# The third gate and value pair moved forward in a fused attention and feed-forward kernel, and ScalarE's masks moved behind its tanh

## The chip, the cores and the metric

The kernel runs on one core of one Trainium2 chip. The metric is device time in microseconds (us) of that core, the median of several executions. The core has five engines that work in parallel, each through its own list of instructions: TensorE (PE in the profile, with its weight loads as PEld) multiplies, VectorE (DVE) and ScalarE (ACT) work on elements, GpSimd (POOL) and SyncE (SP) issue loads and stores here. TensorE writes its results to PSUM, from where VectorE and ScalarE fetch them.

## The reference

A sliding-window attention with distance bias feeds a gated feed-forward block. Batch 8, 8 heads, sequence 576, head size 64, window 128; 4608 tokens of width 512, inner width 1536.

```python
scores = q @ k.T / sqrt(64) - slope[h] * abs(i - j)      # kept where 0 <= i - j < 128
attn = softmax(scores)
x = (attn @ v)                       # heads side by side: 4608 x 512
g = x @ w_gate                       # 4608 x 1536
silu = g * (1 / (1 + exp(-g)))
out = (silu * (x @ w_val)) @ w_out   # 4608 x 512
```

## The kernel before: the parts that matter here

Tokens are worked on in nine blocks of 512 (`n`), the inner width in twelve parts of 128 (`m`). A part has a gate multiplication `pg` and a value multiplication `pv`, each of four matmuls into one PSUM tile of 512 columns. `wide` makes one of them; columns may be done in pieces, and the tile stays in `early` until its last columns are in:

```python
OTHER = {(0, 0, "g"), (0, 0, "v"), (0, 1, "g"), (0, 1, "v")}

def wide(n, m, which, c1=512):
    w, ms = wg_sb if which == "g" else wv_sb, slice(m * P, (m + 1) * P)
    ps, c0 = early.pop((n, m, which), (None, 0))
    if ps is None:
        pool, tag = (ps_a, "a") if (n, m, which) in OTHER else (ps_f, "gv")   # "gv" has 3 buffers, "a" has 4
        ps = pool.tile([P, 512], FP32, name="p" + which, tag=tag)
    for kb in range(NKB):                                                     # NKB = 4
        nc.tensor.matmul(ps[:, c0:c1], w[:, kb, ms], xT[n][:, kb, c0:c1], ...)
    if c1 < 512:
        early[(n, m, which)] = (ps, c1)
    return ps
```

`gate` takes tanh on ScalarE (tile `tt`) and a product on VectorE (`uu`), `val` the product with the value on VectorE (`hT`). Both read PSUM:

```python
def gate(n, m, pg, c0=0, c1=512):
    ...
    nc.scalar.activation(tt, pg[:, c0:c1], AF.Tanh, scale=0.5)
    nc.vector.scalar_tensor_tensor(out=uu, in0=tt, scalar=..., in1=pg[:, c0:c1], op0=ALU.add, op1=ALU.mult)

def val(n, m, pv, c0=0, c1=512):
    ...
    nc.vector.tensor_mul(hT[n][:, m, c0:c1], acted[(n, m)][1][:, c0:c1], pv[:, c0:c1])

def gate_val(n, m):
    c0 = 384 if (n, m) in acted else 0
    gate(n, m, wide(n, m, "g"), c0)
    yield
    val(n, m, wide(n, m, "v"), c0)
    yield
```

The kernel opens with the attention of the first four pieces of 128 tokens, because the first weights arrive then. It multiplies the columns of block 0 as their tokens become ready, for the first three pairs (`begin` makes the pieces up to a column). Before the feed-forward loop starts, the first 384 columns of the first three pairs are in, and those of pairs 0 and 1 have been through `gate` and `val`:

```python
    begin(4, 3)
    gate(0, 0, early[(0, 0, "g")][0], 0, 384)
    x_transposed(FIRST - 1)
    val(0, 0, early[(0, 0, "v")][0], 0, 384)
    later_masks(0, 2)
    gate(0, 1, early[(0, 1, "g")][0], 0, 384)
    val(0, 1, early[(0, 1, "v")][0], 0, 384)
    begin(6, 3)
```

The masks (`m_reg`) are eight exponentials on ScalarE, one for each head. The later attention scores are multiplied with them. Two are made above, the other six between the first steps of the feed-forward loop, and `make_masks` copies them into three further tiles (`m_c`) later:

```python
def later_masks(n, many):
    for h in by_slot[n:n + many]:
        nc.scalar.activation(reg[:, slot(h), :], dist, AF.Exp, scale=-(2.0 ** (-8.0 * (h + 1) / H)))

    # in ffn(), for each block n
    for m in range(NMB):                         # NMB = 12
        for half, _ in enumerate(gate_val(n, m)):
            yield 1.0
            ...
        if n == 1:
            if m in (4, 6, 8, 10):
                for _ in project(0, m // 2 - 2, ps_f, "po", 1):
                    yield 1.0
    ...
    # in everything()
    with tc.manual_schedule(engines=ENGINES[MANUAL]):    # TensorE, VectorE, ScalarE in the order of the program
        first_tiles()
        steps = progress(ffn())
        while (at := next(steps)) < ALONE:               # ALONE = 8
            if at == 2.0:
                nc.scalar.copy(idm2, idm)
            if at in (1.0, 3.0, 4.0):
                later_masks(2 * (1, 3, 4).index(at) + 2, 2)
```

After step 8 a scheduler of the build chooses the order of the instructions on each engine from the dependences, up to step 60 (the end of block 1) on TensorE and throughout on the others. Attention of later tokens and the feed-forward blocks are then mixed. Attention has scores (`ps`, `psc`), exponentials (`ex`, `exc`), products with the masks, products with v (`av`), normalising (`rec`, `x`) and a transpose of x (`px`, copied to `xT`), which the gate of the next block needs. k and q are transposed through `pt`.

The projection of block 0 (`po`) begins with the last rows of `wo_sb`; these weights are loaded in two halves, the last rows first:

```python
def project(n, j, pool, tag, bufs):
    po = pool.tile([P, DM], FP32, name="po", tag=tag, bufs=bufs)     # one buffer
    for m0 in range(0, NMB, 4):
        for i in range(m0, m0 + 4):
            m = NMB - 1 - i if n == 0 else i
            nc.tensor.matmul(po, hT[n][:, m, j * P:(j + 1) * P], wo_sb[:, m, :], ...)
        if m0 + 4 == NMB:
            nc.scalar.mul(osb, po, 0.5)
            ...
    # the loads, on GpSimd's queue behind all other weights
    nc.gpsimd.dma_start(wo_sb[:, 6:12, :], wo2[:, 6:12, :])
    nc.gpsimd.dma_start(wo_sb[:, 0:6, :], wo2[:, 0:6, :])
```

Of the kernel before, what the change touches and what calls it, by code (L numbers as in the profile page):

```python
# [39 lines left out]
def slot(h):  # L40

    return 4 * (h // 4) + 2 * (h % 2) + (h % 4) // 2
# [9 lines left out]
def kernel(  # L52
# [15 lines left out]
    NMB = DFF // P  # L68
# [38 lines left out]
# [3 lines that stand above are left out]
# [282 lines left out]
# [5 lines that stand above are left out]
            pool, tag = (ps_a, "a") if (n, m, which) in OTHER else (ps_f, "gv")  # L397
            ps = pool.tile([P, 512], FP32, name="p" + which, tag=tag)
        for kb in range(NKB):
            nc.tensor.matmul(ps[:, c0:c1], w[:, kb, ms], xT[n][:, kb, c0:c1],  # L400
                             start=(kb == 0 and c0 == 0), stop=(kb == NKB - 1 and c1 == 512),
                             skip_group_check=(n == 0))
# [3 lines that stand above are left out]
# [4 lines left out]
    def gate(n, m, pg, c0=0, c1=512):  # L410

        if (n, m) not in acted:
            acted[(n, m)] = [supool.tile([P, 512], FP16, name=i, tag=i) for i in ("tt", "uu")]
        tt, uu = (t_[:, c0:c1] for t_ in acted[(n, m)])
        if (n, m) in by_silu:
            nc.scalar.activation(tt, pg[:, c0:c1], AF.Silu)
            return
        nc.scalar.activation(tt, pg[:, c0:c1], AF.Tanh, scale=0.5)  # L418
        nc.vector.scalar_tensor_tensor(out=uu, in0=tt, scalar=one if (n, m) == PIN else 1.0,  # L419
                                       in1=pg[:, c0:c1], op0=ALU.add, op1=ALU.mult)  # L420

    def val(n, m, pv, c0=0, c1=512):

        if n not in hT:
            hT[n] = hpool.tile([P, NMB, 512], FP16, name="hT", tag="hT")
        if (n, m) in by_silu:
            nc.vector.scalar_tensor_tensor(out=hT[n][:, m, c0:c1], in0=acted[(n, m)][0][:, c0:c1], scalar=2.0,
                                           in1=pv[:, c0:c1], op0=ALU.mult, op1=ALU.mult)
            return
# [8 lines that stand above are left out]
# [55 lines left out]
    def at_once(fs):  # L493
        for f in fs:
            f()
# [209 lines left out]
    def ffn():  # L705

        for n in range(NBLK):
            if n > 1:
                parts = chain(strassen(n - 1, 0), strassen(n - 1, 1))
            if n == 1:  # L710
                for j in range(PRE):
                    for _ in project(0, j, ps_f, "po", 1):
                        yield 1.0
            if n == SEVEN_FROM:
                break
            due, given = 0, 0
            for m in range(NMB):
                for half, _ in enumerate(gate_val(n, m)):
                    scored[0] = False
                    yield 1.0  # L720
                    due += n > 1 and 2 * m + half in AT
                    while due and not (scored[0] and given % 7 == 1):
                        next(parts)
                        due, given = due - 1, given + 1
                        yield 0.75
                    if n > 1:
                        for _ in range(1 + (len(later) > 3)):
                            if later:
                                later.pop(0)()
# [4 lines that stand above are left out]
                    if m in (4, 6, 8):  # L734
                        weight_sums(m // 2 - 2)
                if n > 0 and m >= 9:
                    (at_once if n == 1 and m < 11 else later.extend)(sums(n, m - 9))
                if n + 1 == SEVEN_FROM:
                    if m == SILU_AT:
                        attention_ends()  # L740
                        by_silu.update((n, i) for i in range(m + 1, NMB))
                    if m in (SILU_AT + 1, SILU_AT + 2):
                        later.extend(gate_val_weight_sums(m - SILU_AT - 1))
                    if m == SILU_AT:
                        later.extend(x_sums(n + 1))
            if n > 1:
                assert next(parts, 0) == 0
        ends = [strassen(NBLK - 1, t) for t in range(2)]
        final = ()
        for n, k, name, which in seven_steps():  # L750
            if k == 0 and n > SEVEN_FROM:
                assert next(parts, 0) == 0
                parts = chain(strassen(n - 1, 0), strassen(n - 1, 1))
            if n == SEVEN_FROM and k in (1, 3, 10, 17):
                later.extend(gate_val_weight_sums(2 + (k + 4) // 7))
            yield 0.5
            if k % 3 == 2 and k < 42:
                next(parts)
                yield 0.75
            if k == 20 and n + 1 < NBLK:  # L760
                later.extend(x_sums(n + 1))
            if k == 35:
                later.extend(sums(n, 0))
            if name == "fourth" and which is not None and which[1] > 3:
                if which == (NBLK - 1, 5):
                    at_once(final)
                else:
                    later.extend(sums(which[0], which[1] - 3))
            if n == NBLK - 1 and k == 40:
                final = sums(n, 2)  # L770
                later.append(final.pop(0))
            for _ in range(2 if len(later) > 4 or k >= 39 or k < 7 else 1):
                if later:
                    later.pop(0)()
            if n == NBLK - 1 and k == 41:
                next(ends[0])
                yield 0.75
        assert next(parts, 0) == 0 and not later

        for t in (1, 0, 1, 0, 0, 0, 1, 0, 0, 1, 1, 1, 1):  # L780
            next(ends[t])
            yield 0.75
# [155 lines left out]
    def progress(steps):  # L938
        total = 0.0
        for size in steps:  # L940
            total += size
            yield total

    def everything():
        nonlocal done
        base = 0
        busy(WARM)
        with tc.manual_schedule(engines=ENGINES[MANUAL]):
            first_tiles()
            done = FIRST  # L950
            steps = progress(ffn())
            while (at := next(steps)) < ALONE:
                if at == 2.0:
                    nc.scalar.copy(idm2, idm)
                if at in (1.0, 3.0, 4.0):
                    later_masks(2 * (1, 3, 4).index(at) + 2, 2)
        fixed = ExitStack()
        for step in steps:
            if step >= FIXED_FROM and fixed is not None:
                fixed.enter_context(tc.manual_schedule(engines=ENGINES["pe"]))  # L960
                fixed, held = None, fixed
            if step == MASKS_AT:
                make_masks()

            b1 = 24 + 3 * PRE

            lead = LEAD if done < X_DMA_FROM - 2 else LEAD + 4
            blk = (0 if step + LEAD < b1 else 1 if step + LEAD < 60
                   else min(NBLK - 1, 2 + int((step + lead - 60) // 34.5)))
            if step < b1:  # L970

                target = base + 1.25 * max(0, step - ALONE) + 1.5 * max(0, step - 16)
            elif step < 60:
                target = base + 32 + SECOND * 8 * (step - b1) / (60 - b1)
            else:
                target = 84 + (step - 57) * RATE / 34.5
            while (n_att < target or done < ready[blk]) and att_step():
                pass
        held.close()
# [33 lines left out]
```

The softmax here doesn't subtract the row's maximum and nothing guards it: scores larger than these inputs give would overflow.

## Time and profile before

| What | Value |
|---|---|
| Device time, median of 3 | 343.38 us (343.19 to 343.41) |
| Span of the profiled execution | 342.1 us, mean granted TensorE clock 0.999 |
| TensorE busy | 330.2 us (97%) |
| VectorE busy | 277.3 us (81%) |
| ScalarE busy | 207.0 us (61%) |
| GpSimd busy | 109.6 us (32%) |
| TensorE busy from 20 to 30 us | 9.20 of 10.00 |
| TensorE busy from 50 to 57 us | 6.56 of 7.00 |

Times in the profile are counted from the start of the span. A row of a timeline gives the start in us, the duration, the engine, the line in the kernel, the operation, what is written from what, and how many instructions were merged; in brackets stands the idle time of the engine just before, with what ended it. TensorE's matmuls overlap at their ends: four of 512 columns show a duration of about 1.03 us but follow each other at 0.86 us. So distances between starts tell more than durations.

### The profile page before, as it was taken

The numbers are of one execution on the slowest core, as the hardware profiler recorded it, in microseconds if no ns is written. First come the engines' busy times: TensorE is split into PE (matmuls) and PEld (weight loads), VectorE is DVE, ScalarE is ACT, GpSimd is POOL, SyncE is SP. The second block draws the span as 40 slices with busy tenths as digits, with TensorE's granted clock in tenths as the row PEclk, the third lists the DMA queues.
The fourth block names the chain that finished last, engine by engine and source line by source line (L and its number), as shares of the span: only waits on it lengthen the run. The fifth ranks groups of instructions, "written<-read, shape, count | busy, mean of one in ns | idle before, by whom it ended". The sixth has DMA issues, their size and how long they took to land.

```text
span 342.1 us, 7787 instructions
## 1 busy us (share of the span) xinstructions
PE 330.2 (97%) x2983; PEld 218.6 (64%) x2983; DVE 277.3 (81%) x652; ACT 207.0 (61%) x412; POOL 109.6 (32%) x136
## 2 busy tenths in 40 slices
PE   7999999999999999999999999999999999999994
PEld 3484445444455665566655655666788878888884
DVE  5477885999798779998899999999855975775683
ACT  3748676565765675666655557463477667676640
POOL 8978672649755176744017000000000000000000
PEclk9999999999999999999999999999999999999999
DMA  9999999999999999999959932041101101011024
GB/s 151 169 180 177 163 173 150 81 132 160 149 173 143 172 166 161 164 162 147 188 125 100 178 35 79 15 77 35 61 10 53 63 0 64 23 41 63 0 71 116
DMA packets 160037, 37.37 MB, mean 109 GB/s; under 512 B 147328, under 2 KB 155648, under 8 KB 160000
## 3 DMA queue, kind: packets, MB, share of 16 engines
q0 software_dynamic: 118336, 18.62, 84.5%
q1 hardware_dynamic: 40976, 17.64, 28.4%
q10 hardware_dynamic: 688, 0.62, 0.6%
q8 instruction: 23, 0.38, 0.5%
q14 instruction: 14, 0.11, 0.1%
HBM read 37.91 MB, written 9.44 MB: 138 GB/s over the span
## 4 chain that ended last, share of the span: by engine, by line
PE 75%; DVE 14%; ACT 6%; issue 3%; DMA 2%; SPq 0%; DVEq 0%
PE po L535 16%; PE pg L400 14%; PE pv L400 14%; PE gX L627 8%; PE av L348 4%; PE gY L627 4%; PE ps L280 3%; PE po L454 2%; PE p L535 2%; DVE hT L430 2%; PE gZ L627 2%; ACT tt L418 2%; ACT ex L286 2%; DVE uu L419 2%; DMA stage<-in_q_dram 2%
## 5 line engine op out<-in xcount | busy, mean ns | idle before, releaser
L400 PE MATMUL pv<-xT,wv_sb 128*128 128x512 f16 (+2 forms) x320 | 76.5, 358 | 0.6 <-DVE uu L419 0.3
L400 PE MATMUL pg<-xT,wg_sb 128*128 128x512 f16 (+2 forms) x320 | 75.8, 358 | 0.3 <-DVE xT L376 0.2
L418 ACT ACTIVATE tt<-pg 128x512 f16<-128x512 f32 (+2 forms) x70 | 41.3, 590 | 47.7 <-PE pg L400 46.6
L286 ACT ACTIVATE ex<-ps 128x512 f16<-128x512 f32 x96 | 50.0, 606 | 10.5 <-PE ps L280 10.5
L419 DVE SCALAR_TENSOR_TENSOR uu<-tt,pg 128x512 f16<-128x512 f16 (+2 forms) x69 | 45.9, 666 | 10.5 <-ACT tt L418 10.3
L430 DVE TENSOR_TENSOR hT<-uu,pv 128x512 f16<-128x512 f16 (+2 forms) x70 | 46.6, 666 | 3.0 <-PE pv L400 1.3
L185 POOL DMA_DIRECT2D va<-in_v_dram x40 | 34.3, 862 | 36.7 <-PE av L348 30.4
L400 PEld LDWEIGHTS <-wv_sb 128*128 128x128 f16 x320 | 28.3, 98 | 25.1 <-issue 3.2
L535 PEld LDWEIGHTS <-hT 128*128 128x128 f16 x384 | 37.0, 98 | 10.6 <-issue 0.8
L400 PEld LDWEIGHTS <-wg_sb 128*128 128x128 f16 x320 | 28.2, 98 | 23.3 <-issue 2.2
L191 POOL DMA_DIRECT2D kn<-in_k_dram x39 | 33.2, 854 | 21.7 <-DMA kT<-kn 11.2
L191 POOL DMA_DIRECT2D qn<-in_q_dram x39 | 33.3, 860 | 15.3 <-DMA va<-in_v_dram 8.8
L535 PEld LDWEIGHTS <-S 128*128 128x128 f16 x288 | 27.3, 98 | 9.0 <-issue 1.4
L292 DVE TENSOR_TENSOR ex<-ex,m_reg 128x1024 f16<-128x1024 f16 x42 | 28.8, 686 | 3.0 <-ACT ex L286 3.0
L351 DVE TENSOR_TENSOR x<-av,rec 128x256 f16<-128x256 f32 x72 | 28.8, 420 | 0.4
L535 PE MATMUL po<-T,S 128*128 128x256 f16 x192 | 26.5, 273 | 0.6 <-DVE S L490 0.3
L535 PE MATMUL po<-T,hT 128*128 128x256 f16 x192 | 26.0, 273 | 0.1
L679 DVE TENSOR_TENSOR hT<-s,v 128x512 f16<-128x512 f16 x18 | 7.6, 423 | 18.5 <-ACT s L678 18.5
L320 ACT ACTIVATE exc<-psc 128x512 f16<-128x512 f32 x40 | 21.3, 609 | 1.9 <-PE psc L316 1.9
L348 PEld LDWEIGHTS <-ex 128*128 128x128 f16 x384 | 17.4, 97 | 4.6 <-issue 1.2
L348 PE MATMUL av<-va,ex 128*128 128x65 f16 x384 | 19.3, 193 | 0.7 <-ACT ex L286 0.7
L280 PE MATMUL ps<-qT,kT 64*128 64x256 f16 x192 | 16.7, 272 | 0.4 <-DVE qT L223 0.2
(134 smaller groups left out, 537.0 us busy)
## 6 DMA issues: line engine op xcount, KB each, us to landing
out_dram<-osb SPq DMA_DIRECT2D x32, 256.0 KB, 2.6
va<-in_v_dram POOLq DMA_DIRECT2D x32, 128.0 KB, 8.1
qn<-in_q_dram POOLq DMA_DIRECT2D x31, 128.0 KB, 8.6
kn<-in_k_dram POOLq DMA_DIRECT2D x31, 128.0 KB, 8.9
wg_sb<-in_moe_w_gate_dram POOLq DMA_DIRECT2D x6, 256.0 KB, 7.7
wv_sb<-in_moe_w_val_dram POOLq DMA_DIRECT2D x6, 256.0 KB, 8.1
wo_sb<-in_moe_w_out_dram POOLq DMA_DIRECT2D x2, 768.0 KB, 9.7
kn<-in_k_dram POOLq DMA_DIRECT2D x8, 64.0 KB, 7.6
```

The lines of the kernel that those rows point to most:

```text
L185: nc.gpsimd.dma_start(va[rank][p0:p1, :, 0:D], src)
L191: nc.gpsimd.dma_start(t_[p0:p1], src)
L286: nc.scalar.activation(e[:, o:o + 2, :], banks[q4][par], AF.Exp, scale=scale)
L292: nc.vector.tensor_mul(e[:, o, :], e[:, o, :], reg[:, o, :])
L348: nc.tensor.matmul(av[:, j, :], w, val, start=(n == 0), stop=(n == len(todo) - 1))
L351: nc.vector.tensor_mul(x[:, 4 * half:4 * half + 4, :], av[:, :, 0:D], rec.broadcast_to([P, 4, D]))
L400: nc.tensor.matmul(ps[:, c0:c1], w[:, kb, ms], xT[n][:, kb, c0:c1], start=(kb == 0 and c0 == 0), stop=(kb == NKB - 1 and c1 == 512), skip_ ...
L418: nc.scalar.activation(tt, pg[:, c0:c1], AF.Tanh, scale=0.5)
L419: nc.vector.scalar_tensor_tensor(out=uu, in0=tt, scalar=one if (n, m) == PIN else 1.0, in1=pg[:, c0:c1], op0=ALU.add, op1=ALU.mult)
L430: nc.vector.tensor_mul(hT[n][:, m, c0:c1], acted[(n, m)][1][:, c0:c1], pv[:, c0:c1])
L535: nc.tensor.matmul(dst, a[:, m, cols], b[:, m, :], start=(start and m == 0), stop=(m == HM - 1), skip_group_check=True)
L627: nc.tensor.matmul(dst[:, i, :], w[:, kb, c0 + i * P:c0 + (i + 1) * P], a[:, kb, :], start=(start and i == 0 and kb == 0), stop=(i == 1 an ...
```

## The change

The last 128 columns of the third pair were multiplied after those of the first and second pairs. Their PSUM tiles have no reader yet, while those of the first two pairs are being read by VectorE (the first 384 columns). The change multiplies them right behind the last columns of the first gate, in the time in which TensorE waits for these readers. It also lets the tanh operations of the second and third gates go ahead of masks on ScalarE: only one of the six later masks stays ahead of them, two follow the third gate, three the fourth. The number and size of all operations stay as they are.

```diff
             due, given = 0, 0
-            for m in range(NMB):
+            if n == 0:
+                gate(0, 0, wide(0, 0, "g"), 384)
+                yield 1.0
+                third = [wide(0, 2, which) for which in "gv"]
+                yield 1.0
+                val(0, 0, wide(0, 0, "v"), 384)
+                yield 1.0
+                gate(0, 1, wide(0, 1, "g"), 384)
+                yield 1.0
+                val(0, 1, wide(0, 1, "v"), 384)
+                yield 1.0
+                gate(0, 2, third[0])
+                val(0, 2, third[1])
+                yield 1.0
+            for m in range(0 if n else 3, NMB):
                 for half, _ in enumerate(gate_val(n, m)):
 ...
                 if at == 2.0:
                     nc.scalar.copy(idm2, idm)
-                if at in (1.0, 3.0, 4.0):
-                    later_masks(2 * (1, 3, 4).index(at) + 2, 2)
+                if at in (3.0, 6.0, 7.0):
+                    later_masks(*{3: (2, 1), 6: (3, 2), 7: (5, 3)}[int(at)])
```

## The prediction

> **What bounds the kernel now.** I read the page's slices first, then each engine's timeline from 23 to 58 us, then the busy time by stage, and last the issue times of the loads. TensorE is the bound nearly everywhere, so a stage's worth is the TensorE gap that it removes.
>
> ```profile
> PE   7999999999999999999999999999999999999994
> 70.00:80.00 10.00, 9.92 (x70) 4.73 (x69) 9.89 (x21) 7.09 (x14) 4.71 (x7) 1.00 2.25 142
> 80.00:90.00 10.00, 9.76 (x87) 4.62 (x85) 9.96 (x27) 5.53 (x11) 8.10 (x11) 1.00 2.12 163
> ```
>
> The last two rows give busy us of PE, PEld, DVE, ACT and POOL: from 70 to 90 VectorE is as full as TensorE (19.85 of 20).
>
> TensorE where the change is made, then VectorE's and ScalarE's rows of the same stretch (start, us, engine, line, operation, tiles, count, and in brackets the idle time before and its releaser):
>
> ```profile
> 23.59 0.38 PE L400 MATMUL pg<-xT,wg_sb 128*128 128x128 f16 x4 [0.16 <-DVE xT L376]
> 24.05 0.38 PE L400 MATMUL pv<-xT,wv_sb 128*128 128x128 f16 x4
> 24.51 0.38 PE L400 MATMUL pg<-xT,wg_sb 128*128 128x128 f16 x4
> 25.10 0.38 PE L400 MATMUL pv<-xT,wv_sb 128*128 128x128 f16 x4 [0.21 <-DVE hT L430]
> 25.32 0.39 PE L400 MATMUL pg<-xT,wg_sb 128*128 128x128 f16 x4
> 25.55 0.39 PE L400 MATMUL pv<-xT,wv_sb 128*128 128x128 f16 x4
> ...
> 27.74 1.02 PE L400 MATMUL pv<-xT,wv_sb 128*128 128x512 f16 x4 [0.27 <-DVE uu L419]
> ```
>
> ```profile
> 23.45 0.54 DVE L430 TENSOR_TENSOR hT<-uu,pv 128x384 f16<-128x384 f16 x1
> 23.91 0.55 DVE L419 SCALAR_TENSOR_TENSOR uu<-tt,pg 128x384 f16<-128x384 f16 x1
> 24.50 0.55 DVE L430 TENSOR_TENSOR hT<-uu,pv 128x384 f16<-128x384 f16 x1
> ```
>
> ```profile
> 25.15 1.32 ACT L109 ACTIVATE m_reg<-stage 128x256 f16<-128x256 f32 x4
> 26.38 0.59 ACT L418 ACTIVATE tt<-pg 128x512 f16<-128x512 f32 x1
> ```
>
> A group of four 128-column multiplications that waits for nothing takes 0.22 us from start to start (25.32, 25.55). The three groups from 24.05 stand 0.46 to 0.59 apart. Each starts just as VectorE finishes reading the same PSUM tile: 24.05 after 23.99, 24.51 after 24.46, 25.10 after 25.05. The two from 25.32 on are the third pair, on tiles that nobody reads yet.
>
> Then GpSimd's rows for the load of the output weights, and TensorE's first uses of them (po):
>
> ```profile
> 42.26 0.82 POOL L911 DMA_DIRECT2D wo_sb<-in_moe_w_out_dram  x1 [0.85 <-DMA va<-in_v_dram]
> ...
> 53.46 0.87 POOL L191 DMA_DIRECT2D qn<-in_q_dram  x1 [2.93 <-DMA wo_sb<-in_moe_w_out_dram]
> ```
>
> ```profile
> 52.06 0.39 PE L454 MATMUL po<-wo_sb,hT 128*128 128x512 f16 x1
> ...
> 54.28 1.03 PE L454 MATMUL po<-wo_sb,hT 128*128 128x512 f16 x4
> ...
> 57.09 1.02 PE L400 MATMUL pg<-xT,wg_sb 128*128 128x512 f16 x4
> ```
>
> The load at 42.26 brings rows 0 to 5 of wo_sb. GpSimd's 53.46 row waited for its semaphore, so it lands at about 53.4. Block 0 uses rows 11 to 6 first, so the seventh po is the first that needs it; it ran third in the group at 54.28, at about 54.7, and waited for nothing. The margin is 1.3 us. 57.09 is the start of block 1.
>
> **What the Trainium skill says.** "PSUM — Partial Sum Buffer", section "PSUM bank collisions raise a hardware error", tells kernels to guard PSUM by bank, as two engines collide even in disjoint columns of one. That is why columns 384 to 511 wait for a reader of columns 0 to 383; the 0.05 to 0.06 us between VectorE's ends and TensorE's starts agree. The same page, section "Engine vs sequencer instructions", says that matmuls start and complete in program order and that ScalarE's and VectorE's queues are strict first in, first out. So tanh behind masks waits for them (26.38, directly behind four masks), and a po whose weights are missing would hold everything behind it; no row before shows the latter. "DMA: Bandwidth & Descriptors", section "Two DMAs through the same engine are not ordered", says that completion semaphores tell when data has landed; I read 53.46 so.
>
> **The change part by part.** No work is added or removed. I take the new instruction order from the changed program and the durations from the rows above.
>
> *1. Third pair moved forward.* Its eight multiplications, 0.45 us (25.32 to 25.77), go behind the first gate at 23.59. The value group then starts at 24.25, its reader done at 23.99; the second gate stays at 24.51 and the second value at 25.10, tied to VectorE. The fourth gate starts at 25.32 instead of 25.77: **-0.45**.
>
> *2. Masks behind tanh.* In the new order ScalarE does tanh (128) at 24.01, the identity copy (0.19 start to start), one mask (0.31), the second 128-column tanh at 24.93 when its gate is finished, and the third gate's tanh at 25.10 instead of 26.38. VectorE's product with it, behind two short pairs, ends at about 26.54 instead of 27.69. The fourth value needs that buffer. TensorE reaches it at 25.32 + 0.865 + 12 x 0.055 = 26.85, without a wait, against 27.74: **-0.89** there, step 1 included.
>
> *3. From 27 to 50.* The masks only move, so ScalarE reaches the fifth gate's tanh at about 29.4 (30.11 before) and the sixth's at 32.45 (32.51): it is again the engine behind. Following the buffers, I get an advance of 0.7 around 33 and 0.45 near 40, where the tenth gate waits for VectorE until 39.65 (40.11 before). **-0.45** is what reaches 50.
>
> *4. The output weights.* The scheduler uses the advance to put six po multiplications before the sixteen score multiplications of about 51 to 52, and the seventh right behind those sixteen, ahead of the last eight scores. Before, the same place held the first po. TensorE gets there at about 52.5. The loads do not come earlier: each of these issues waited for an older load. So TensorE stands until 53.4, some **0.9 us**, with scores behind it.
>
> From 53.45: po, 4 scores, po, 4 scores, po are 5 x 0.22 = 1.1, to 54.55; av (0.24), po, av, to 55.25. The last av result comes 0.19 later, the reciprocal takes 0.17 (rec 0.36 for two), x 0.39: 55.95. Then px, k and q transposes (0.11 + 0.44) and two po (0.43) end at 56.97. The second x, behind a mask product (0.60) and itself 0.42, ends at 56.9. Its px is finished at 57.24, the ScalarE copy at 57.83. Block 1 starts at **57.9 against 57.09: +0.8**.
>
> *5. Work done ahead.* By then four po of the next projection are done as well, which ran after 72.5 before. 4 x 0.215 = 0.86: **-0.86** for TensorE from there on.
>
> *6. VectorE.* It, too, begins block 1 later by 0.8 us and isn't relieved of anything. From 70 to 90 it is full, and TensorE waits for its x there. The new order puts about 0.65 us more TensorE work ahead of the last of these transposes, which hides most. I leave **+0.1 to +0.3**.
>
> Sum at 95: +0.8 - 0.86 + 0.2 = +0.14. Steps 1 to 3 are not added, since step 4's landing time replaces them. From there TensorE is dense (49.4, 49.97 and 49.94 busy of each 50 us to 250) and its order fixed, so this reaches the end: 343.38 + 0.14 = **343.5**.
>
> **Rivals.**
> *The advance survives.* If the output weights land before TensorE needs them, step 4 has no stall. For it: the opening gaps are real, and loads could finish a little sooner. Against it: the landing at 53.4 is set by a chain of loads. The time would then be -0.45 and some idle time of 50 to 57 filled (7 - 6.56 = 0.44): about 342.5.
> *VectorE is the bound of 60 to 92.* Then the 0.8 of step 4 stays whole and the 0.86 of step 5 becomes waits. For it: 19.85 of 20 us. Against it: VectorE idles 1.7 us at 94 (its wait for tanh), so a part is caught up. It gives 344.2.
> *Nothing opens at all,* because VectorE's readers, not tanh, free the opening's buffers. Rows 27.00 and 26.38 speak against it; it would give 343.4.
>
> **Range and chances.** Step 4 could be wrong by 0.5 us either way and step 6 by 0.4; the shuffled ScalarE and VectorE orders after 60 add perhaps 0.3. Range 342.7 to 344.3. 2% is 6.9 us, over seven times the largest single term, so within 2% gets 0.98, and either side 0.01.
>
> **What would show it.** Right: the fourth gate at about 25.3 and the fourth value near 26.9; the first po near 50; a TensorE gap at 52 to 53.4 that ends with a po released by a load of wo_sb; block 1 at about 57.9; eight po instead of twelve at 72 to 76. Wrong: a fourth value still near 27.7 fells step 2; no gap before 53.4, or a landing well before it, fells step 4 and leaves the first rival; waits for VectorE between 80 and 93 that sum to over 0.8 us make it the second.

## The result and the profile after

| What | Before | After |
|---|---|---|
| Device time, median of 6 | 343.12 us (342.84 to 343.41) | 344.62 us (343.99 to 345.87) |
| Ratio, with 95% interval | | 1.0045 (1.0026 to 1.0064) |
| Span of the profiled execution | 342.1 us | 343.1 us |
| TensorE busy | 330.2 us | 330.2 us |

The changed kernel is slower by 1.5 us. By size that is within 2%, but 344.62 lies 0.3 above the predicted range. TensorE does the same 330.2 us of work; what came is idle time. The page's slices and the busy time by stage of the kernel after (busy us of PE, PEld, DVE, ACT, POOL) show where:

```profile
PE   7998998999999999999999999999999999999995
```

```profile
50.00:57.00 7.00, 5.64 (x64) 3.00 (x63) 3.83 (x10) 4.83 (x9) 3.60 (x5) 1.00 2.02 168
70.00:80.00 10.00, 9.90 (x72) 4.64 (x71) 9.89 (x23) 7.11 (x14) 5.48 (x7) 1.00 2.55 145
80.00:90.00 10.00, 9.31 (x80) 4.52 (x78) 9.77 (x26) 4.79 (x10) 9.97 (x14) 1.00 2.04 177
```

From 50 to 57 TensorE is busy for 5.64 us (6.56 before), from 80 to 90 for 9.31 (9.76 before). Behind 97 us the distance between the two stays what it is there (1.29 us at 97, 1.31 at TensorE's last group). The two profiled executions differ by 1.0 in span, as what follows TensorE's last group, the last stores, is 0.3 shorter in the later one; the medians differ by 1.5.

TensorE's timeline of the kernel after, by rows as before:

```profile
23.22 0.61 PE L400 MATMUL pg<-xT,wg_sb 128*128 128x128 f16 x8 [0.16 <-DVE xT L376]
23.66 0.61 PE L400 MATMUL pv<-xT,wv_sb 128*128 128x128 f16 x8
24.14 0.38 PE L400 MATMUL pg<-xT,wg_sb 128*128 128x128 f16 x4
24.73 0.38 PE L400 MATMUL pv<-xT,wv_sb 128*128 128x128 f16 x4 [0.20 <-DVE hT L430]
24.95 1.03 PE L400 MATMUL pg<-xT,wg_sb 128*128 128x512 f16 x4
...
27.34 0.40 PE L218 MATMUL pt<-idm,qn 128*128 128x128 f16 x4 [0.91 <-DMA qn<-in_q_dram]
27.57 1.03 PE L400 MATMUL pv<-xT,wv_sb 128*128 128x512 f16 x4
...
50.07 1.25 PE L454 MATMUL po<-wo_sb,hT 128*128 128x512 f16 x5
...
51.58 0.91 PE L316 MATMUL psc<-qT,kT 64*128 64x128 f16 x16
53.61 0.38 PE L454 MATMUL po<-wo_sb,hT 128*128 128x512 f16 x1 [1.12 <-DMA wo_sb<-in_moe_w_out_dram]
53.92 0.40 PE L316 MATMUL psc<-qT,kT 64*128 64x128 f16 x4
54.25 0.39 PE L454 MATMUL po<-wo_sb,hT 128*128 128x512 f16 x1
54.57 0.39 PE L316 MATMUL psc<-qT,kT 64*128 64x128 f16 x4
54.90 0.39 PE L454 MATMUL po<-wo_sb,hT 128*128 128x512 f16 x1
...
58.52 1.02 PE L400 MATMUL pg<-xT,wg_sb 128*128 128x512 f16 x4
...
73.97 1.90 PE L454 MATMUL po<-wo_sb,hT 128*128 128x512 f16 x8
75.71 0.42 PE L348 MATMUL av<-va,ex 128*128 128x65 f16 x8
...
86.52 0.29 PE L374 MATMUL px<-idm,x 128*128 128x128 f16 x2 [0.62 <-DVE x L351]
...
97.48 1.02 PE L400 MATMUL pg<-xT,wg_sb 128*128 128x512 f16 x4
```

The rows of the kernel before that answer to the last of these:

```profile
75.14 0.42 PE L348 MATMUL av<-va,ex 128*128 128x65 f16 x8
...
86.36 0.28 PE L374 MATMUL px<-idm,x 128*128 128x128 f16 x2 [0.24 <-DVE x L351]
...
96.19 1.02 PE L400 MATMUL pg<-xT,wg_sb 128*128 128x512 f16 x4
```

This execution reached the changed part 0.37 us earlier than the one before (23.22 against 23.59). The difference is there before the changed part (the first gate comes between 22.96 and 23.61 in the runs below), so rows of the opening are compared by their distance from the first gate. The first group holds eight multiplications now, the first gate's and the third's. The fourth gate starts at 24.95 (25.77 before). Then a q load is late by 0.91. The first po starts at 50.07 (52.06 before), the seventh waits 1.12 us for its weights, and block 1, which starts at 57.09 before, starts at 58.52.

VectorE's, ScalarE's and GpSimd's rows of the same kernel:

```profile
25.78 0.68 DVE L419 SCALAR_TENSOR_TENSOR uu<-tt,pg 128x512 f16<-128x512 f16 x1
```

```profile
24.56 0.77 ACT L418 ACTIVATE tt<-pg 128x128 f16<-128x128 f32 x2
25.21 0.72 ACT L109 ACTIVATE m_reg<-stage 128x256 f16<-128x256 f32 x2
```

```profile
42.64 0.83 POOL L925 DMA_DIRECT2D wo_sb<-in_moe_w_out_dram  x1 [0.82 <-DMA va<-in_v_dram]
...
53.86 0.88 POOL L191 DMA_DIRECT2D qn<-in_q_dram  x1 [2.63 <-DMA wo_sb<-in_moe_w_out_dram]
```

The two tanh stand together at 24.56 (the second is the third gate's, of 512 columns; the row gives the shape of the first), and the third gate's product starts at 25.78, so the masks did go behind. The load that TensorE waits for was issued at 42.64 (42.26 before), 0.4 later and not earlier, as GpSimd's queue has its own chain of waits.

At 97 us the account of the two traces is: block 1 starts later, +1.43; the four po that are already done, -0.86 (the av behind po is at 75.71 against 75.14, so +0.57 is left); between 76 and 97, +0.72. The gate of block 2 comes at 97.48 against 96.19: +1.29.

### The profile page after: what moved, and what is told of

It reads as the page before. It is cut to its first block, busy times and chain, and to the rows that moved or that the text cites. A ratio compares the mean times of both kernels' runs of the same rounds, so it can differ in the third digit from the quotient of the medians.

```text
span 343.1 us, 7785 instructions
## 1 busy us (share of the span) xinstructions
PE 330.2 (96%) x2983; PEld 218.9 (64%) x2983; DVE 277.2 (81%) x652; ACT 207.5 (60%) x412; POOL 109.8 (32%) x136
## 4 chain that ended last, share of the span: by engine, by line
PE 66%; DVE 14%; DMA 9%; POOL 5%; ACT 3%; issue 2%; DVEq 0%; POOLq 0%
PE po L535 16%; PE pg L400 12%; PE pv L400 12%; PE gX L627 8%; PE gY L627 4%; DMA wo_sb<-in_moe_w_out_dram 3%; PE av L348 3%; DMA qn<-in_q_dram 3%; DMA va<-in_v_dram 3%; PE ps L280 2%; PE p L535 2%; PE gZ L627 2%; DVE uu L419 2%; DVE hT L430 2%; POOL va L185 2%
```

## The experiments

Theory A: the change wins what the prediction says, and two obstacles take more than that: TensorE stands for the output weights near 53 us, and VectorE's full queue (busy for 25.31 us of the 26 from 60 to 86 in the changed kernel) takes back the four po. Each ratio is against the kernel before on the same chip.

### The weight load split, in both kernels

```diff
-    nc.gpsimd.dma_start(wo_sb[:, 0:6, :], wo2[:, 0:6, :])
+    nc.gpsimd.dma_start(wo_sb[:, 3:6, :], wo2[:, 3:6, :])
+    nc.gpsimd.dma_start(wo_sb[:, 0:3, :], wo2[:, 0:3, :])
```

Rows 5 to 3, which the seventh po needs first, come as a load of their own. TensorE's order doesn't change. In the changed kernel (after_split):

> The changed kernel with the second load of the output weights (rows 0 to 5) split in two loads of three rows each; all instructions on TensorE keep their order. Theory A (the seventh po waits for that load, and everything behind it with it): rows 3 to 5 land near 51.7 us, so the wait of 1.1 us is gone, block 1 starts near 57.4 instead of 58.5, and the time falls by 0.9 to 1.2 us, to 343.3 to 343.7. Rival B (the other order of scores, products and transposes that the scheduler chose is what costs, through VectorE between 80 and 95 us): the wait is gone but the time stays at 344.2 to 344.6.

Measured: 343.48 us, ratio 1.0007 (1.0000 to 1.0013). In the kernel before (before_split):

> The kernel before with the same split load, as a control. Theory A: TensorE did not wait for this load before, so nothing changes: 343.1, within 0.2. If the split by itself is worth something (earlier weights, other shares of the DMA engines), it shows here.

Measured: 343.35 us, ratio 1.0001 (0.9993 to 1.0009). The split is worth about 1 us where the wait is and nothing where it is not. TensorE's timeline of after_split:

```profile
51.84 0.39 PE L454 MATMUL po<-wo_sb,hT 128*128 128x512 f16 x1
...
56.78 1.02 PE L400 MATMUL pg<-xT,wg_sb 128*128 128x512 f16 x4
...
73.97 0.42 PE L348 MATMUL av<-va,ex 128*128 128x65 f16 x8
...
84.78 0.28 PE L374 MATMUL px<-idm,x 128*128 128x128 f16 x2 [0.61 <-DVE x L351]
...
95.75 1.02 PE L400 MATMUL pg<-xT,wg_sb 128*128 128x512 f16 x4
```

The seventh po (51.84) waits for nothing and block 1 starts at 56.78, 0.6 before what I expected; in before_split that is 56.85. So of the opening's advance the only thing left at block 1 is the four po, and still the time is no better than before. At the av (73.97) the kernel is 0.94 ahead of before_split (74.91), at the gate of block 2 (95.75) only 0.21 ahead (95.96): 0.73 is lost between the two. The px at 84.78 waits 0.61 for VectorE.

### Each half of the change alone

part1 has the third pair moved, with the masks in the old places. part2 has the old order of pairs and only this edit:

```diff
-                if at in (1.0, 3.0, 4.0):
-                    later_masks(2 * (1, 3, 4).index(at) + 2, 2)
+                if at in (2.0, 6.0, 7.0):
+                    later_masks(*{2: (2, 1), 6: (3, 2), 7: (5, 3)}[int(at)])
```

> Only the third pair's last columns moved forward; masks and tanh on ScalarE in the order of before, and with it the later order of TensorE is that of before. Theory A: the fourth gate starts 0.45 us earlier, but the fourth value still waits for the third gate's tanh behind four masks, so it stays where it was and the gain is lost there: 343.1, within 0.2; no early po, no wait for the output weights. Rival C (the move itself lengthens the kernel): about 344.5. Rival D (its 0.45 us is kept): 342.7.

Measured: 343.22 us, ratio 0.9997 (0.9989 to 1.0005).

> Only the masks moved behind tanh on ScalarE; the third pair's last columns stay where they were. The later order of TensorE has the po multiplications as early as in the changed kernel. Theory A: the fourth value starts about 0.4 us earlier than before, then TensorE waits for the output weights until 53.5 as in the changed kernel, and the time is 344.3 to 344.8. Rival D: 342.7 (the advance is kept).

Measured: 344.41 us, ratio 1.0036 (1.0022 to 1.0051). TensorE's timeline of part1, then of part2:

```profile
24.98 1.03 PE L400 MATMUL pg<-xT,wg_sb 128*128 128x512 f16 x4
...
27.41 1.04 PE L400 MATMUL pv<-xT,wv_sb 128*128 128x512 f16 x4 [0.60 <-DVE uu L419]
```

```profile
26.49 1.02 PE L400 MATMUL pv<-xT,wv_sb 128*128 128x512 f16 x4
...
53.23 0.38 PE L454 MATMUL po<-wo_sb,hT 128*128 128x512 f16 x1 [1.64 <-DMA wo_sb<-in_moe_w_out_dram]
```

The third pair alone gains its 0.45 at the fourth gate and loses it 2.4 us later to the tanh that still stands behind the masks. The masks alone bring the fourth value to 3.53 after the first gate (26.49 - 22.96; 4.15 before), 0.6 earlier where I had expected 0.4. The scheduler puts the po forward in this kernel too, and the whole stall comes with it. The loss belongs to this half.

### The q load that came late

The 0.91 us at 27 us could be a loss of its own. The changed kernel was run once more (after_again), and with this q load issued ahead of a v load (after_q5):

```diff
-    load(4)
+    load_qk(4)
     load_qk(5, "q")
+    load_v(4)
```

> The changed kernel once more, on the same chip and beside the same runs of the kernel before as the two that follow. The late landing of one q load (TensorE waits 0.91 us for it at about 27 us in the first profile) differed from kernel to kernel. If it belongs to this order of loads: again 344.3 to 344.9 us with a q wait of 0.7 to 1.0. If it is scatter from one loading of the program to the next: a q wait of 0.2 or none, and 343.9 to 344.3.

Measured: 344.35 us, ratio 1.0039 (1.0023 to 1.0054). TensorE's timeline of after_again:

```profile
26.37 0.71 PE L218 MATMUL pt<-idm,qn 128*128 128x128 f16 x8
26.92 1.03 PE L400 MATMUL pv<-xT,wv_sb 128*128 128x512 f16 x4
```

No wait for q stands here, so the late landing differs between two executions of one kernel. The time is no lower for it: it stays in the range that I had given for the case with the wait.

> The changed kernel with the sixth head's q load issued ahead of the v load of the head before it; nothing else. Theory A (the wait for the output weights ends at their landing, so whatever comes before it costs nothing): the q wait at 27 us goes, the wait near 53 us grows by as much as is gained, and the time falls by no more than the landing comes earlier: 343.9 to 344.5 us. Rival (the q wait is a part of the loss in its own right): 343.5 to 343.8.

Measured: 344.21 us, ratio 1.0039 (1.0021 to 1.0056). TensorE's timeline of after_q5:

```profile
53.16 0.38 PE L454 MATMUL po<-wo_sb,hT 128*128 128x512 f16 x1 [1.51 <-DMA wo_sb<-in_moe_w_out_dram]
...
58.06 1.02 PE L400 MATMUL pg<-xT,wg_sb 128*128 128x512 f16 x4
```

TensorE arrives earlier (its sixteen scores start at 50.74 instead of 51.58), so the wait is longer, 1.51 us, and ends at 53.16; in after_again it was 0.99 and ended at 53.20. Counted from the first gate, block 1 starts at 35.30 in the first profile, with the q wait, and at 35.09 here, without it: of the 0.91 won ahead of the landing, 0.7 are given back at it. In these profiles the wait of kernels with the early po ends between 52.60 and 53.61.

### VectorE's work between 76 and 82 us moved away

The third part of the weight sums (`weight_sums(2)`: two L478, an L480, an L481, about 2 us) is first read at 102 us. It is now called behind the last product of block 1, and one of its operands (`one_more[-1]`) comes from a one-column operation on that product, so that it can't run earlier:

```diff
-            nc.vector.scalar_tensor_tensor(out=t_[:, k, :], in0=a[:, k, :], scalar=one_more[0],
+            nc.vector.scalar_tensor_tensor(out=t_[:, k, :], in0=a[:, k, :], scalar=one_more[-1],
 ...
-                    if m in (4, 6, 8):
+                    if m in (4, 6):
                         weight_sums(m // 2 - 2)
+                    if m == NMB - 1:
+                        one_more.append(supool.tile([P, 1], FP32, name="one2", tag="pin2", bufs=1))
+                        nc.vector.scalar_tensor_tensor(out=one_more[1], in0=hT[1][:, m, 0:1], scalar=0.0,
+                                                       in1=one_more[0], op0=ALU.mult, op1=ALU.add)
+                        weight_sums(2)
```

With the split load, in the changed kernel (split_late):

> The changed kernel with the weight load split and, in addition, the third part of the weight sums (two 2-row differences of T1 and T3 and one each of T2 and T4, about 2 us of VectorE's time between 76 and 82) tied to the last product of block 1, so that it runs after about 95 us. Theory A (VectorE is full from 59 to 85 us and takes back the four output multiplications done ahead): the px wait of about 0.6 us near 85 us disappears, block 2 starts about 0.6 us earlier than in the split kernel, 342.6 to 343.0 us in all. Rival (the gain is lost to something else, for example ScalarE's tanh or the third sums now being late for their own users near 100): the time stays at 343.3 to 343.7.

Measured: **342.50 us, ratio 0.9977 (0.9967 to 0.9986)**, faster than both kernels and 0.1 under my range. Without the split (after_late):

> The changed kernel with only the third part of the weight sums moved behind the last product of block 1; the weight load is not split. Theory A: the wait for the output weights stays (about 1.1 us near 53 us, block 1 at about 58.4), the px waits of 80 to 93 us go, 343.7 to 344.1 us, 0.6 to 0.8 under the changed kernel's 344.6. Rival (the px waits only mirror the late start of block 1): no change, 344.5 to 344.7.

Measured: 343.42 us, ratio 1.0004 (0.9997 to 1.0011), 0.3 better than I expected. Its wait for the output weights ended at 52.60, the earliest of all; I cannot say whether that is more than scatter. In the kernel before, without and with the split:

> The kernel before with only the third part of the weight sums moved. Theory A: TensorE misses only 0.24 us of the ten between 80 and 90 here, so at most that can come back: 343.0 to 343.3 us. Rival (VectorE holds block 1 in this kernel as well): 342.6 or less.

Measured: 343.06 us, ratio 0.9993 (0.9984 to 1.0002).

> The kernel before with the weight load split and the third part of the weight sums moved back, that is with both remedies and without the change. Theory A (both remedies only take away what the change ran into): 343.0 to 343.3 us, 0.6 above the changed kernel with the same two. Rival (the remedies are worth 0.8 by themselves, and the change nothing): 342.4 to 342.7.

Measured: 343.29 us, ratio 1.0001 (0.9993 to 1.0010). So both remedies bring the kernel before nothing that these runs resolve; with them, the change is worth 343.29 - 342.50 = 0.8 us. VectorE's timeline of after_split, then VectorE's and TensorE's of split_late:

```profile
81.63 0.42 DVE L481 TENSOR_TENSOR T<-wo_sb,T 128x512 f16<-128x512 f16 x1
...
82.97 0.42 DVE L488 TENSOR_TENSOR S<-hT 128x512 f16<-128x512 f16 x1
83.31 0.17 DVE L350 RECIPROCAL rec<-av 128x4 f32<-128x4 f32 x1
83.40 0.39 DVE L491 TENSOR_TENSOR S<-hT,S 128x512 f16<-128x512 f16 x1
83.71 0.68 DVE L419 SCALAR_TENSOR_TENSOR uu<-tt,pg 128x512 f16<-128x512 f16 x1
84.31 0.41 DVE L351 TENSOR_TENSOR x<-av,rec 128x256 f16<-128x256 f32 x1
```

```profile
81.78 0.42 DVE L491 TENSOR_TENSOR S<-hT,S 128x512 f16<-128x512 f16 x1
82.81 0.18 DVE L350 RECIPROCAL rec<-av 128x4 f32<-128x4 f32 x1 [0.60 <-PE av L348]
83.02 0.42 DVE L351 TENSOR_TENSOR x<-av,rec 128x256 f16<-128x256 f32 x1
```

```profile
26.92 1.04 PE L400 MATMUL pv<-xT,wv_sb 128*128 128x512 f16 x4
...
74.33 0.42 PE L348 MATMUL av<-va,ex 128*128 128x65 f16 x8
...
83.71 0.28 PE L374 MATMUL px<-idm,x 128*128 128x128 f16 x2
```

In the first, no row has brackets: VectorE comes from one operation to the next, and the reciprocal is taken 0.90 us after the eight av that it reads were done (82.41). In the second VectorE has waited 0.60 for that av: it is TensorE that is waited for. The px then follows without a wait, at 83.71, and TensorE is busy for 9.90 us from 80 to 90 instead of 9.31.

The distances between three points of TensorE's timeline separate the causes (us; the kernels of a row agree to 0.01 where one figure stands):

| Kernels | First gate to block 1 | From there to the av near 75 | From there to the gate of block 2 |
|---|---|---|---|
| before, before_split, part1 | 33.50 | 18.05 | 21.05 |
| before_late, before_split_late | 33.50 | 18.05 | 20.92 |
| after, part2, after_q5 | 35.09 to 35.30 | 17.19 | 21.77 |
| after_split | 33.53 | 17.19 | 21.78 |
| after_late | 34.54 | 17.19 | 20.93 |
| split_late | 33.53 | 17.19 | 20.92 |

after_again has 17.19 and 21.76 in the last two columns, and 35.86 in the first, where its profile shows a granted clock of 0.84 from 50 to 57 us. The first column holds the stall, and the split ends it. The second holds the four po done ahead. The third grows by 0.72 in every kernel with the early po and the sums in their old place, whether block 1 starts late or not, and falls to 20.92 with and without the early po when the sums are moved. Of the 0.86 between after_split and split_late there, 0.58 is idle time of TensorE; the other 0.28 is busy time, for as many multiplications in another order.

One rival is left. In after_split a sum and a gate product (83.40, 83.71) stand between the reciprocal and x, which starts 1.00 us after it; in the kernel before (83.95, 84.16) and in split_late x follows at 0.21. An order of VectorE with x right behind its reciprocal might end the wait as well, with the sums in their old place. No run has it. So it is shown that moving the sums is enough, but not whether it is VectorE's load or the scheduler's order on VectorE that has to change.

Last, split_late with the q load moved (split_late_q5):

> The kernel split_late with the load of the sixth head's q issued ahead of the v load of the head before it, against the q wait of 0.2 to 0.9 us at about 26.6 to 27.3 us. If that wait is on the path to block 1: 0.2 to 0.4 us under split_late. If block 1's start is set elsewhere (the scores and ScalarE between 27 and 50 us): the same as split_late to 0.1.

Measured: 342.45 us, ratio 0.9978 (0.9966 to 0.9990), as split_late. TensorE's timeline:

```profile
53.69 0.38 PE L454 MATMUL po<-wo_sb,hT 128*128 128x512 f16 x1 [0.20 <-DMA wo_sb<-in_moe_w_out_dram]
...
55.62 0.40 PE L218 MATMUL pt<-idm,qn 128*128 128x128 f16 x4 [0.21 <-DMA qn<-in_q_dram]
```

Its opening is 0.65 us ahead of split_late's (first gate at 22.96 against 23.61), which is not the edit's doing: the fourth value comes 3.31 after the first gate in both, as split_late had no wait for this q either. So the run doesn't test that wait. What it shows, in one execution that at 343.05 lies 0.6 above the median, is an earlier start that meets the other part of the weight load and then a q load: block 1 starts at 57.23 against 57.14.

## Why the prediction was right or wrong

Two steps failed. Step 4 had the right wait but was too small by 0.63 us. Step 6 took it that other work of TensorE would hide the wait for VectorE, and was too small by 0.52. Together they are the 1.15 us by which the account of the traces missed (+1.29 against +0.14).

*1. Third pair moved forward*: right. Counted from the first gate, the fourth gate comes at 1.73 (24.95 - 23.22) against 2.18 before: -0.45 as predicted. part1 shows it alone.

*2. Masks behind tanh*: right, and the wait is gone, but in the first profile a q load took its place (the fourth value comes 4.35 after the first gate, 4.15 before). In split_late, where q is there, the fourth value comes 3.31 after the first gate instead of 4.15: -0.84, predicted -0.89. I had looked at the buffers and not at the loads that the moved-up transposes need. It cost nothing that after_again and after_q5 resolve.

*3. From 27 to 50*: predicted -0.45. Counted from the first gate, the q transposes near 50 come at 26.61 before, 26.48 in the first profile with its q wait, and 25.86 in after_split: -0.13 and -0.75. In the changed kernel it didn't matter, as stated, since step 4 replaces it.

*4. The output weights*: the wait came where it was predicted, **the size +0.8 was wrong: +1.43**. The wait ended at 53.61 instead of 53.45 (+0.16). From there to the first av I took five groups at 0.22 us, 1.1 in all. The rows have 0.31 to 0.33 from po to scores to po, and 1.51 in all: +0.41. Scores are multiplications of 64 rows, po of 128. The profile before had the spacing already, in the same pattern (po at 52.06, scores at 52.38, po at 52.71); I had used the spacing of a run of equal groups. The remaining +0.05 is spread. "PSUM — Partial Sum Buffer" of the Trainium skill, section "Engine vs sequencer instructions", says that matmuls start and complete in program order. This trace agrees, with 1.12 us in which eight scores, which need no weights, stood behind one po. after_split takes the wait away, and the time falls from 344.35 to 343.48.

*5. Work done ahead*: right. +1.43 at block 1 has become +0.57 at the av near 75.

*6. VectorE*: TensorE does wait for x, but **the hiding that I counted on failed, and +0.1 to +0.3 was +0.72**. I gave the late start of block 1 as the cause and held that TensorE's extra work before the last transposes hides it. after_split has no late start and loses the same. With 0.86 us less to do before 75, TensorE comes to the transposes sooner relative to VectorE, whose work is unchanged and back to back; three gate multiplications (0.65 us) do stand ahead of the px at 86.52, and it still waits 0.62. So 0.72 of the 0.86 are gone by 97: 0.43 as idle time of TensorE (1.34 us in its last stretch of the table, 0.91 before) and 0.29 as busy time, for as many multiplications in another order. How much of the wait is due to VectorE's load and how much to its order is open (the rival above). This was my second rival. Its number was 344.2, with step 4 at +0.8 whole; with +1.43 it gives 344.8, near the 344.6 measured. The sign that I had named for it, waits of over 0.8 us between 80 and 93, did not come: they sum to 0.62. The limit was set too high, as the 0.29 of busy time shows no wait. My reason against it, that VectorE idles near 94 and catches up, failed: the wait is at 86.5, before that. split_late and after_late show the part of VectorE: with 2 us of VectorE's work moved behind 95 us, the wait for x goes and the time falls by 0.98 and 0.93 (342.50 against 343.48, 343.42 against 344.35).

The rival *The advance survives* fell with the row at 53.61. *Nothing opens at all* fell with the fourth value in part2 and split_late. Whether the third pair's move adds anything to the 0.8 us that the change is worth with both remedies is open: no run has the masks alone with the remedies.

## What to carry to other kernels

When a scheduler makes the order, an earlier opening can pull a consumer ahead of a load that has its own timetable, as it did here with the seventh po; look up the landing time of each load against the new place of its first reader, and split the load by what is read first. Work done ahead on the bounding engine can come to nothing if the next engine to fill up isn't relieved too (here 0.72 of 0.86 us): look for the stretch where that engine runs back to back, and move from there what nobody waits for. When you add up a stretch, take the spacing of the pattern that will run there, with its alternation of shapes, and not that of a row of equal operations.

## What the runs showed that I had not expected

A po between groups of four 64-row scores takes 0.31 to 0.33 us from start to start of each, while groups of 128 rows of the same length follow each other at 0.22. The same q load, issued at about the same time (17.24 to 17.49 us), held TensorE until 27.34 us in one execution and until 26.65, 26.34 or not at all in others, with no effect on the time that the runs resolve.
